# An mLSTM cell followed by a squared-ReLU feed-forward network: order of turning, weighting and transfers, and the place of one weight rounding

## The chip, the cores and the metric

The kernel runs on one core of a Trainium2 chip. The metric is the device time of one execution in microseconds (us); before the change it is 506.15 us as the median of six runs (504.21 to 507.88). TensorE multiplies matrices, VectorE (DVE in the profile), ScalarE (ACT) and GpSimd (POOL) work element by element, and SyncE (SP) issues nearly all transfers (DMAs). Each engine works through its own list of instructions in the order in which the kernel wrote them, and waits on semaphores for what other engines or transfers deliver.

## The reference

Two stages, in float32. The first is an mLSTM cell over 4 batches, 8 heads, 768 steps and a head dimension of 40:

```
m_new  = max(f[t] + m, i[t])
f_stab = exp(f[t] + m - m_new);  i_stab = exp(i[t] - m_new);  m = m_new
C = f_stab * C + i_stab * outer(v[t], k[t])
n = f_stab * n + i_stab * k[t]
y[t] = sigmoid(o[t]) * (C @ q[t]) / max(|n . q[t]|, 1)
```

The second takes the result as 3072 tokens of width 320 (batch and step as rows, head and dimension as columns):

```
h   = max(x @ w_in, 0)        # w_in  320 x 2048
out = (h * h) @ w_out         # w_out 2048 x 320
```

## The kernel before

**Chunks.** The recurrence is cut into 24 chunks of 128 steps (six for each batch), s = 0 to 23, each for all eight heads. Inside a chunk the cell is an attention with decays: the scores of keys against queries (`scores`, L445), times the weights exp(A + b) below the diagonal (`weighted`, L467, which multiplies the scores out of PSUM by the weights W and leaves P in W's place), then P times the values and the carried state C times the decayed queries (`attend_turned`, L542, L551 and L561).

**What a chunk needs.** `load_A` (L352) broadcasts a row of accumulated decays from DRAM to all 128 partitions, 512 KB in one transfer, into one of two buffers A_bc; `decays` (L387, ScalarE) takes its exponential for the queries, `mask` (L377, GpSimd) cuts the upper triangle, `weigh` (L401, ScalarE, eight exponentials) makes W. Keys and queries are needed turned, dimension on the partitions. From chunk 7 on this goes by way of DRAM: `pair_up` (L305, four transfers) copies k and q into rows, `load_squares` (L327, four transfers) reads them back as 32 x 32 squares into one of two buffers kqT, and `turn_kq` (L334, VectorE) turns every square. `scale_q` (L515) multiplies the queries by the decays.

**After a chunk.** `store_num` (L580) writes the numerators to DRAM and `load_num` (L585, four transfers) reads them back turned; `normalise_turned` (L597 to L606) divides and gates; `store_rows` (L632) and `load_rows` (L637) do the same for the result x, which `turn_squares` (L644) turns for the network.

**The network.** Tokens go in groups of two chunks, g = 0 to 11. Groups 0 and 1 take plain products (L674, L685); from group 2 on the first layer is done with a fast scheme of seven products over 2 x 2 blocks (`ffn1_begin`, `ffn1_open`, `ffn1_close`; L841, and L890 for the last 64 rows), and from group 1 on the second layer likewise (`ffn2_fast`, L765; sums on VectorE at L760, L781). In `ffn1_open` VectorE adds two products out of PSUM (L873, L875), in `ffn1_close` TensorE adds further products into the same banks, and VectorE ends with L908 to L911.

**Weights.** w_in and w_out come as 64-bit words and are rounded to float32 in 18 pieces by `Rounding`: `words` on ScalarE (L210, L212), `join` on VectorE (L221, L225, L226) and GpSimd (L230), each `join` also issuing the transfer of a later piece (L200). `step` does one `join` and keeps `words` one piece ahead.

**The order.** The schedule is written out by hand. A first loop, u = 0 to 7, does chunks 2 to 5 with the first layer of groups 0 and 1; `NEXT[u]` says how many pieces are rounded by the end of each u, and `WIN_SUMS` adds sums of weights after it (u = 7: L826). The second loop goes over units n, four for each chunk: `s = 6 + n // 4`, `at = n % 4`. `parts` gives each unit a quarter of a layer of the network: four quarters of the second layer, or (`fast`) of the first. `LAST[n]` is the number of rounded pieces by the end of unit n. Even chunks from 8 on do the scores of two chunks: their own at at = 0 and those of the next, odd one at at = 1. At at = 1 the transfers on SP are written in a row; at at = 2 others follow. Chunks 6 and 7 use a simpler order of transfers than chunks from 8 on.

Of the kernel before, what the change touches and what calls it, by code (L numbers as in the profile page):

```python
# [29 lines left out]
def kernel(  # L30
# [259 lines left out]
    def load_parts(s):  # L290
        d = st.setdefault(s, {})
        kq, va = d["kq"], d["va"] = kq_b[s % NKQ], va_b[s % NKQ]
        return (kq[:, 0, :, :D], k), (kq[:, 1, :, :D], q), (va[:, :, :D], v)
# [42 lines left out]
    def load_o(s):  # L336
        b, c = divmod(s, NB)
        r, (s0, s1) = next((r, (a, z)) for r, (a, z) in enumerate(RUNS) if a <= s < z)
        if s == s0:
            st["og", r] = ld.tile([P, 4, H, D], F32, name="og")  # L340
        og = st.setdefault(s, {})["og"] = st["og", r][:, s - s0]
        nc.sync.dma_start(og, o_gate[b, :, c * P : (c + 1) * P, :].rearrange("h p d -> p h d"))

    def sigmoid(s):
        nc.scalar.activation(st[s]["og"], st[s]["og"], AF.Sigmoid)
# [71 lines left out]
    def bank(o=False):  # L417
        if o == "h":
            t = ps_h.tile([P, W], F32, name="h_ps")
        else:  # L420
            t = ps_o.tile([P, W], F32, name="tp", tag="o_ps") if o else ps_at.tile([P, W], F32, name="tp", tag="at")
        return t[:].rearrange("p (j t) -> p j t", j=PR)
# [12 lines left out]
    def scores(s, o=(False, False)):  # L435
        d = st[s]

        sc = [bank(o[i]) for i in range(2)]
        d["sc"] = sc
        if s >= KQ_SQ:  # L440
            for j in range(PR):
                for keys in HALVES:
                    for i in range(2):
                        rows = slice(DP * i, DP * i + D)
                        nc.tensor.matmul(  # L445
                            sc[i][keys, j, :], lhsT=d["kT"][rows, j, keys], rhs=d["qT"][rows, j, :], start=(j == 0),
                            stop=True, skip_group_check=True,
                        )
            return
        for j in range(PR):  # L450
            for i in range(2):
                rows = slice(DP * i, DP * i + D)
                nc.tensor.matmul(  # L453
                    sc[i][:, j, :], lhsT=d["kT"][rows, j, :], rhs=d["qT"][rows, j, :], start=True, stop=True,
                )

    def weighted(s):
        d = st[s]
        d["P"] = []
        for i in range(2):  # L460
            heads = slice(i, H, 2) if s < KQ_SQ else slice(PR * i, PR * (i + 1))
            t = d["W"][:, heads, :]
            if s < W_IN:
                at = 2 * H * P + W * (2 * (s % 2) + i)
                t = flat_c[:, at : at + W].rearrange("p (j t) -> p j t", j=PR)
            d["P"].append(t)
            nc.vector.tensor_tensor(t, d["sc"][i], d["W"][:, heads, :], op=ALU.mult)  # L467
# [410 lines left out]
    def ffn1_rows(g, q, first):  # L878
        xT, xs = st["xT", g], st["xs"]
        X, Y, V, Z = st["f1"]  # L880
        lo, hi = HALVES
        pairs = (
            ((X, lo, xT[lo, 0, 2, :], False), (Y, hi, xT[hi, 1, 2, :], first)),
            ((V, lo, xT[lo, 1, 2, :], first), (Z, hi, xs[hi, 1, :], False)),
        )
        for pair in pairs:
            for n in range(4):
                for cols in HALVES:
                    for to, rows, rhs, start in pair:
                        nc.tensor.matmul(  # L890
                            to[cols, n, :], lhsT=w_in2[rows, 4 * q + n, cols], rhs=rhs,
                            start=(start and n == 0), stop=True, skip_group_check=True,
                        )
# [29 lines left out]
    def do(f, s):  # L923
        if 0 <= s < NT:
            f(s)

    def score(s):
        scores(s)
        weighted(s)


    zeros = consts.tile([P, 16], BF16)
    nc.vector.memset(zeros[:], 0.0)
# [12 lines left out]
    def load_part(s, i):  # L946
        b, c = divmod(s, NB)
        dst, src = load_parts(s)[i]
        nc.sync.dma_start(dst, src[b, :, c * P : (c + 1) * P, :].rearrange("h p d -> p h d"))
# [60 lines left out]
    rounding.step()  # L1010


    NEXT = (5, 8, 10, 11, 12, 13, 14, 15)
    WIN_SUMS = {5: 0, 6: 1, 7: 3}
    for u in range(8):
        s = 2 + u // 2
# [45 lines left out]
        if u < 4:  # L1062
            load_o(4 + u)
        while rounding.done < NEXT[u]:
            rounding.step()
# [17 lines left out]
    for g in range(1, NG):  # L1083
        parts += [(2, g, i) for i in range(4)]
        if g + 2 < NG:
            parts += [(1, g + 2, i) for i in range(4)]
    LAST = (16, 17, 18, 18, 18)
    assert LAST[-1] == len(pieces)
    for n, (which, g, i) in enumerate(parts):
        s, at = 6 + n // 4, n % 4  # L1090
        if n == 5:
            brought.close()
            late = ctx.enter_context(tc.tile_pool(name="late", bufs=1, side="right"))
        even = s >= 8 and s % 2 == 0
        fast = which == 1
        if at == 0:
            if s < 8 or even:
                do(score, s)
            if even:
                do(turn_kq, s + 1)  # L1100
        if at == 1:
            if even:
                do(lambda s: scores(s, ("h", "h")), s + 1)
            if fast:
                ffn1_rows(g, 0, True)
            do(attend_turned, s)
            do(decays, s + 1)
            do(mask, s + 1)
            if n > 4 and not even and not fast:
                do(turn_kq, s + 1)  # L1110
            do(decay_C, s + 1)
            if s > X_SQ and not fast:
                do(turn_squares, s - 1)
            do(store_num, s)
            if s >= 8:
                do(load_A, s + 2)
                do(lambda s: load_part(s, 0), s + 4)
                do(load_num, s)
                if not even:
                    do(load_squares, s + 2)  # L1120
                do(lambda s: load_part(s, 2), s + 4)
                if s < 20:
                    load_o(s + 4)
            else:
                do(load, s + 4)
                do(load_num, s)
            do(pair_up, s + 3)
        if 5 <= n < 8:
            sums_of_weights(n - 5)
        if n == 6:  # L1130
            sums(1, slice(0, NPAIR), (1, 2))
        if n == 8:
            sums_of_weights(3)
            sums(1, slice(0, NPAIR), (3,))
        if n == 9:
            sums(1, slice(0, NPAIR), (4,))
        if which == 2 and i == 3 and g == NG - 2:
            sums(g + 1, slice(0, NPAIR), (2,))
        if which == 2 and g > 1 and i < 2:
            sums(g, slice(0, NPAIR), (3 + i,))  # L1140
        if n == 0:
            ffn1_begin(g)
            sums_of_x(g)
            sums_of_win(2)
        if at == 3 and s >= 8 and s % 2 == 0 and s // 2 - 1 < NG:
            sums_of_x(s // 2 - 1)
        if at == 2 and not fast:
            if n > 4:
                do(scale_q, s + 1)
        if at == 3:  # L1150
            if s % 4 == 3:
                for r in range(s + 1, min(s + 5, NT)):
                    sigmoid(r)
        if fast:
            if i % 2:
                ffn1_close(g, i // 2, i == 1)
                if at == 1 and g > 2:
                    do(turn_kq, s + 1)
                    do(turn_squares, s - 1)
            else:  # L1160
                ffn1_open(g, i // 2)
                if i == 0 and g > 2:
                    sums(g - 1, slice(0, NPAIR), (2,))
            if at == 2 and g > 2:
                do(scale_q, s + 1)
        elif g == 0:
            ffn2(g, *divmod(i, 2))
        else:
            ffn2_fast(g, i)
        if at == 2:  # L1170
            do(lambda s: weigh(s, masked=True), s + 1)
            ffn1_square()
            if n < 4:
                do(turn_kq, s + 1)
                do(scale_q, s + 1)
            if even:
                do(weighted, s + 1)
            do(normalise_turned, s)
            do(store_rows, s)
            if s < 8 or even:  # L1180
                do(load_squares, s + 2)
            do(load_rows, s)
            if s < 8:
                do(load_A, s + 2)
        if at == 0:
            ffn1_square()
        if n < 5:
            while rounding.done < LAST[n]:
                rounding.step()
# [30 lines left out]
```

## Time and profile before

| what | value |
|---|---|
| median of six runs | 506.15 us |
| the profiled execution | 504.89 us |
| its span, first to last instruction | 503.1 us |
| TensorE matmul busy | 492.7 us (98%) |
| VectorE busy | 351.5 us (70%) |
| ScalarE busy | 249.0 us (49%) |
| GpSimd busy | 115.8 us (23%) |
| 16 DMA engines busy, SP's queue | 64.1% |
| granted TensorE clock | 1.0 |

The profile is of one execution. Times in it run from the first instruction. A line such as L334 is the line of the kernel text whose instruction is meant. PE is TensorE, PEld its weight loads, SPq SyncE's queue, on which each row is the issue of transfers and not their duration. Idle time of an engine is put down to the instruction or transfer that ended it. The page's row of the busy tenths shows TensorE at 9 in nearly all of the 40 slices after the first; the wall between the loops lies at some 97 us, chunk 8 begins at 137 us, and after 437 us only products of the second layer are left.

### The profile page before, as it was taken

To read this page: it belongs to the slowest core of one execution; us is meant where nothing else is said; L and a number is where in the kernel's file an instruction comes from. 1 tells how busy PE (TensorE), PEld (TensorE's weight loads), DVE (VectorE), ACT (ScalarE), POOL (GpSimd) and SP (SyncE) were. 2 spreads that over 40 slices of the span, in tenths; PEclk is the share of its full clock that TensorE was granted. 3 is DMA by queue.
4 is the path that set the end of the run, shared out by engine and by line. 5 is a ranking of instruction groups with operands and counts; after the bars stand their busy time and mean duration, and the time that the engine had idled before them with its cause. 6 is when DMAs were issued, how large, how long until landed. Compare 5 with 4: busy or idle time off the path is not lost.

```text
span 503.1 us, 13823 instructions
## 1 busy us (share of the span) xinstructions
PE 492.7 (98%) x5640; PEld 456.9 (91%) x5641; DVE 351.5 (70%) x646; ACT 249.0 (49%) x492; POOL 115.8 (23%) x138
## 2 busy tenths in 40 slices
PE   9988999989999999999999999999999999999997
PEld 4877878887689999999999999999999999999997
DVE  8588968779976776686876866767867856735441
ACT  3867888763532651672651680551771650423400
POOL 3356743232313021013013031013013030020000
PEclk9999999999999999999999999999999999999999
DMA  9999899855577867767867867867864622200000
GB/s 187 210 232 216 240 216 176 209 98 98 147 153 143 155 149 141 152 154 141 150 154 142 165 151 131 163 146 139 159 159 84 147 60 59 75 15 14 1 27 26
DMA packets 238238, 67.74 MB, mean 135 GB/s; under 512 B 185600, under 2 KB 232704, under 8 KB 238176
## 3 DMA queue, kind: packets, MB, share of 16 engines
q1 hardware_dynamic: 238080, 66.68, 64.1%
q8 instruction: 44, 0.72, 0.6%
q10 hardware_dynamic: 96, 0.20, 0.1%
q14 instruction: 18, 0.15, 0.1%
HBM read 54.56 MB, written 17.86 MB: 144 GB/s over the span
## 4 chain that ended last, share of the span: by engine, by line
PE 90%; DVE 5%; DMA 2%; ACT 1%; issue 1%; SPq 1%; POOL 0%; DVEq 0%; POOLq 0%
PE h_ps L765 33%; PE h_ps L841 25%; PE h_ps L890 8%; PE h_ps L674 4%; PE numT L551 4%; PE hp L490 2%; PE h_ps L445 2%; PE tp L445 1%; PE numT L542 1%; PE idle L938 1%; PE h_ps L685 1%; PE tp L453 1%; PE dC L483 1%; DMA va<-in_v_dram 1%; PE tp L430 1%; PE h_ps L711 1%
## 5 line engine op out<-in xcount | busy, mean ns | idle before, releaser
L377 POOL TENSOR_SCALAR_AFFINE_SELECT A_bc<-A_bc 128x1024 f32<-128x1024 f32 x22 | 25.9, 1176 | 134.3 <-ACT kq L387 86.4
L765 PE MATMUL h_ps<-T,S 128*128 128x160 f32 x352 | 51.4, 299 | 0.0
L871 ACT COPY r_sb<-h_ps 128x512 f32<-128x512 f32 x18 | 10.5, 585 | 80.1 <-PE h_ps L841 80.1
L765 PE MATMUL h_ps<-w_out,g 128*128 128x160 f32 x336 | 49.2, 303 | 0.0
L765 PEld LDWEIGHTS h_ps<-T,S 128*128 128x128 f32 x352 | 49.0, 190 | 0.0
L765 PEld LDWEIGHTS h_ps<-w_out,g 128*128 128x128 f32 x336 | 46.1, 190 | 1.4 <-issue 1.2
L401 ACT ACTIVATE A_bc<-A_bc,b_T 128x128 f32<-128x128 f32 x144 | 44.0, 389 | 4.2 <-POOL A_bc L377 3.9
L781 DVE TENSOR_TENSOR y_sb<-y_sb,h_ps 128x160 f32<-128x160 f32 x44 | 14.1, 320 | 43.5 <-PE h_ps L765 43.3
L841 PE MATMUL h_ps<-lent_t,w_in 128*128 128x128 f32 x320 | 42.5, 276 | 1.4 <-DVE r_sb L873 1.4
L841 PE MATMUL h_ps<-xT,w_in 128*128 128x128 f32 x320 | 42.8, 278 | 0.0
L841 PEld LDWEIGHTS h_ps<-lent_t,w_in 128*128 128x128 f32 x320 | 38.9, 192 | 1.6 <-DVE r_sb L873 1.6
L841 PEld LDWEIGHTS h_ps<-xT,w_in 128*128 128x128 f32 x320 | 38.9, 192 | 1.1 <-issue 0.7
L890 PE MATMUL h_ps<-xT,w_in 64*64 64x128 f32 x960 | 39.4, 273 | 0.0
L841 PE MATMUL h_ps<-lent_t 128*128 128x128 f32 x320 | 39.0, 275 | 0.0
L841 PEld LDWEIGHTS h_ps<-lent_t 128*128 128x128 f32 x320 | 37.3, 192 | 0.0
L890 PEld LDWEIGHTS h_ps<-xT,w_in 64*64 64x64 f32 x960 | 34.6, 133 | 2.4
L568 DVE STREAM_TRANSPOSE tn<-numT 128x256 f32<-128x256 f32 x36 | 15.8, 449 | 25.8 <-PE numT L551 25.8
L413 POOL TENSOR_TENSOR vw<-va,A_bc 128x328 f32<-128x328 f32 x15 | 11.9, 794 | 83.9 <-issue 40.5
L674 PE MATMUL h_ps<-xT,w_in 128*128 128x256 f32 x128 | 29.6, 383 | 1.2 <-POOL w_in L230 0.6
L908 DVE TENSOR_TENSOR r_sb<-r_sb,h_ps 128x512 f32<-128x512 f32 x20 | 13.7, 686 | 20.7 <-PE h_ps L841 14.3
L674 PEld LDWEIGHTS h_ps<-xT,w_in 128*128 128x128 f32 x128 | 23.6, 190 | 5.0 <-POOL w_in L230 1.0
L765 PE MATMUL h_ps<-w_out,g_c 128*128 128x160 f32 x192 | 28.0, 302 | 0.0
(188 smaller groups left out, 1078.6 us busy)
## 6 DMA issues: line engine op xcount, KB each, us to landing
A_bc<-a_rows SPq DMA_DIRECT2D x22, 512.0 KB, 5.3
num_rows<-tn SPq DMA_DIRECT2D x18, 256.0 KB, 2.6
kq<-num_rows SPq DMA_DIRECT2D x72, 64.0 KB, 3.4
raw<-in_moe_w_out_dram SPq DMA_DIRECT2D x7, 640.0 KB, 4.4
kqT<-kq_rows SPq DMA_DIRECT2D x34, 128.0 KB, 3.4
kq<-in_k_dram SPq DMA_DIRECT2D x24, 160.0 KB, 5.6
va<-in_v_dram SPq DMA_DIRECT2D x24, 160.0 KB, 4.2
og<-in_o_gate_dram SPq DMA_DIRECT2D x24, 160.0 KB, 3.5
```

The source lines that it names most:

```text
L377: nc.gpsimd.affine_select(A[:], A[:], compare_op=ALU.is_ge, fill=-1e30, base=0, pattern=[[0, H], [1, P]], channel_multiplier=-1,)
L401: nc.scalar.activation(d["W"][:, i * n + h, :], A[i][:, h, :], AF.Exp, bias=b_T[:, b, c, i * n + h : i * n + h + 1],)
L413: nc.gpsimd.tensor_tensor(d["vw"][:], d["va"][:], d["W"][:, :, P - 1 : P].to_broadcast([P, H, D1]), op=ALU.mult,)
L445: nc.tensor.matmul(sc[i][keys, j, :], lhsT=d["kT"][rows, j, keys], rhs=d["qT"][rows, j, :], start=(j == 0), stop=True, skip_group_check=True,)
L551: nc.tensor.matmul(numT[i][halves[g], e, :], lhsT=va_w[s % NKQ][:, h * D1 : h * D1 + DP], rhs=d["P"][h % 2][:, h // 2, :] if s < KQ_SQ els ...
L568: nc.vector.transpose(to[:, 2 * i : 2 * i + 2], numT[i][:, :2, :].rearrange("p c t -> p (c t)"))
L674: nc.tensor.matmul(hs[i][:, n, :], lhsT=w_in[:, a, fb * P : (fb + 1) * P], rhs=xT[:, :, a, :], start=(n == 0 and a == 0), stop=False,)
L765: nc.tensor.matmul(to, lhsT=lhsT[:, p], rhs=rhs[:, p, :], start=(start and p == 0), stop=(p == NPAIR - 1), skip_group_check=True,)
L781: add = lambda to, a, b: nc.vector.tensor_tensor(to, a, b, op=ALU.add)
L841: nc.tensor.matmul(to[:, n, :], lhsT=lhsT[:, 4 * q + n, :], rhs=rhs, start=(start and n == 0), stop=True, skip_group_check=True,)
L890: nc.tensor.matmul(to[cols, n, :], lhsT=w_in2[rows, 4 * q + n, cols], rhs=rhs, start=(start and n == 0), stop=True, skip_group_check=True,)
L908: tt(U2[:], U2[:], Y[:], op=ALU.add)
```

## The change

Four edits, all in the order of instructions:

- `NEXT[7]` is 16 in place of 15 and `LAST[0]` is 17 in place of 16: one step of rounding is written at the end of u = 7, so that units 0 and 2 have one each and unit 1 has none.
- In even chunks from 8 on, `turn_kq(s + 1)` stands between `scores(s)` and `weighted(s)`, not behind both (`score`, a helper that called both, is gone).
- In chunks from 8 on, `load_A(s + 2)` is issued behind `load_part(s + 4, 0)`, `load_num(s)` and, in odd chunks, `load_squares(s + 2)`, not ahead of them.
- Chunk 7 takes the order of transfers that the later odd chunks have: its `load_squares(9)` and `load_A(9)` are issued at at = 1, not at at = 2, and its v behind them.

```diff
-    def score(s):
-        scores(s)
-        weighted(s)
...
-    NEXT = (5, 8, 10, 11, 12, 13, 14, 15)
+    NEXT = (5, 8, 10, 11, 12, 13, 14, 16)
...
-    LAST = (16, 17, 18, 18, 18)
+    LAST = (17, 17, 18, 18, 18)
...
         if at == 0:
             if s < 8 or even:
-                do(score, s)
+                do(scores, s)
             if even:
                 do(turn_kq, s + 1)
+            if s < 8 or even:
+                do(weighted, s)
...
             do(store_num, s)
-            if s >= 8:
-                do(load_A, s + 2)
+            if s > 6:
                 do(lambda s: load_part(s, 0), s + 4)
                 do(load_num, s)
                 if not even:
                     do(load_squares, s + 2)
+                do(load_A, s + 2)
                 do(lambda s: load_part(s, 2), s + 4)
-                if s < 20:
+                if 8 <= s < 20:
                     load_o(s + 4)
             else:
                 do(load, s + 4)
...
-            if s < 8 or even:
+            if s < 7 or even:
                 do(load_squares, s + 2)
             do(load_rows, s)
-            if s < 8:
+            if s < 7:
                 do(load_A, s + 2)
```

## The prediction

> **What bounds the kernel now.** I read the page's busy times first, then the list of waits for the matmul engine alone, then the timelines round its two late waits on all queues, and last one steady pair of chunks, to see what margin the moved work has.
>
> ```profile
> PE 492.7 (98%) x5640; PEld 456.9 (91%) x5641; DVE 351.5 (70%) x646; ACT 249.0 (49%) x492; POOL 115.8 (23%) x138
> ```
>
> TensorE is busy for 492.7 of 503.1 us. The diff adds and removes no matmul and leaves the matmuls in their order, so only idle TensorE time can be won. The waits of TensorE, with what ended them:
>
> ```profile
> PE h_ps L841 <- DVE r_sb L873: 1.4, 1, 1.4
> PE tp L652 <- ACT g L698: 1.2, 1, 1.2
> PE dC L483 <- DVE g_c L467: 1.1, 1, 1.1
> ...
> PE h_ps L445 <- DVE kqT L334: 0.8, 1, 0.8
> ```
>
> All nine rows of that list add up to 7.3 us. L652, L483, both L674 and the start-up idle lie before 66 us, ahead of every edit. Two are left within reach: the first and the last shown. After 144 us no row is left. The first, on VectorE and then TensorE (start, duration, instruction, idle before and its releaser):
>
> ```profile
> 109.50 0.68 DVE L911 TENSOR_TENSOR g_c<-r_sb,h_ps 128x512 f32<-128x512 f32 x1
> 110.10 0.49 DVE L221 TENSOR_SCALAR mag<-mag 128x640 f32<-128x640 f32 x1
> 110.62 0.49 DVE L225 TENSOR_SCALAR mag<-mag 128x640 int32<-128x640 int32 x1
> 111.15 0.82 DVE L226 SCALAR_TENSOR_TENSOR mag<-raw,mag 128x640 int32<-128x640 int32 x1
> 111.89 0.68 DVE L873 TENSOR_TENSOR r_sb<-h_ps,r_sb 128x512 f32<-128x512 f32 x1
> 112.63 1.16 PE L841 MATMUL h_ps<-lent_t,w_in 128*128 128x128 f32 x8 [1.39 <-DVE r_sb L873]
> ```
>
> Unit 1's rounding (L221 to L226) stands ahead of the addition L873, which must have read its PSUM bank before TensorE may add to it. The second, at chunk 8, with the transfer queue (SPq) first:
>
> ```profile
> 128.30 1.75 SPq L585 DMA_DIRECT2D kq<-num_rows  x4
> ...
> 136.40 2.94 SPq L327 DMA_DIRECT2D kqT<-kq_rows  x4
> ...
> 142.43 0.47 SPq L352 DMA_DIRECT2D A_bc<-a_rows  x1
> 138.52 1.29 DVE L467 TENSOR_TENSOR A_bc<-tp,A_bc 128x512 f32<-128x512 f32 x2 [1.18 <-PE tp L445]
> 142.47 1.25 DVE L334 STREAM_TRANSPOSE kqT<-kqT 128x1024 f32<-128x1024 f32 x1 [2.66 <-DMA kqT<-kq_rows]
> 143.77 1.16 PE L445 MATMUL h_ps<-kqT 40*64 40x128 f32 x30 [0.83 <-DVE kqT L334]
> ```
>
> Chunk 9's squares are issued at 136.40, land after 142, VectorE waits 2.66 us to turn them, and TensorE, done with its products at 142.94, waits 0.83.
>
> **What the Trainium skill says.** "PSUM — Partial Sum Buffer", section Engine vs sequencer instructions: the queues of ScalarE, VectorE and GpSimd are strictly first in, first out, and matmuls start in program order. Both waits above are of this kind. "DMA: Bandwidth & Descriptors", section Anatomy of one DMA: a semaphore is waited for on the issuing sequencer, before dispatch. So what stands behind a waiting issue on SP waits too; here L585 starts at 128.30, 3.8 us after its chunk's store at 124.49. The same page, section Queues, rings and completion order: each DMA engine consumes a ring in order. That store had the 512 KB broadcast of A (issued 122.81) in front of it; the median landing of such a store is 2.6 us. This agrees, without being proof.
>
> **The rounding, worked out.** The step that unit 0 did goes to the end of u = 7; unit 0 then does the one that unit 1 did, and unit 1 does none. In unit 1, VectorE loses 0.49 + 0.49 + 0.82 us; by starts it is 111.89 - 110.10 = 1.79. L873 then starts at 110.10 and ends at 110.8, before TensorE comes at 111.24: the wait of **1.39** goes entirely, with 0.4 to spare. Where the step lands:
>
> ```profile
> 93.63 1.22 DVE L826 TENSOR_TENSOR lent_t<-w_in,lent_t 128x1024 f32<-128x1024 f32 x1
> 96.94 1.29 DVE L467 TENSOR_TENSOR A_bc<-tp,A_bc 128x512 f32<-128x512 f32 x2 [2.10 <-PE tp L453]
> ```
>
> VectorE waits 2.10 us before L467 for the scores; the step takes 1.8 to 1.9, so L826 moves to 95.5 and L467 stays. On ScalarE its two passes (0.81 + 0.79, starts 0.7 apart, so 1.4) come at 93.7, after L704, where 1.55 us of idle wait for the matmul L685 to end at 95.3. Their raw piece was issued at 85.51 (median landing 4.4 us). GpSimd's addition (1.54) falls into its idle from 93.5 to 105. Cover gone by half a microsecond: L826's sum is not read before 106.5, but L698's ReLU may free PSUM that TensorE takes at 96.8; at worst 0.5 us. I take 0; range 0 to +0.5.
>
> What is late next: chunk 7's weighting (L467) ended at 122.80 against TensorE's L551 at 122.84, no margin. TensorE will come at 121.45. VectorE: L873 and L875 to 111.5, L334 to 112.75, L515 to 113.45, L597 to L606 (1.7) to 115.15, the remaining rounding 1.8 to 116.95, L908 to L911 2.4 to 119.35, L467 to 120.6. Margin 0.85. The reload of the numerators that L597 needs has all landed by 112.6, so it does not wait.
>
> **Chunk 7's transfers.** All on SP. The four squares of chunk 9 leave their place behind x_sb (136.40) for that behind L585; the broadcast of A for chunk 9 follows them (was 142.43), then v (0.67), the four kq_rows and the output. L585 starts about 126.3: its store moves with TensorE to 123.1 and takes 3.2, less than the 3.8 above because A for chunk 8 is issued some 2 us sooner, behind an x_sb that is sooner. L585 takes 1.75 and the squares 2.94: issued from 128.1 to 131.0. From first issue to last landing they took 6 us before (136.40 to 142.4), which gives 134.1. VectorE reaches the turn at 135.8, and TensorE wants the scores at 142.94 - 1.39 = 141.55, so even 5 us more would be hidden: the **0.83** goes. What has been pushed back: kq_rows, from 130.1 to 132.1, are read by squares issued at 159; the output, 2 us later, holds one of three y_sb. A for chunk 9 is issued 11 us sooner. All 0.
>
> **Turning kq first in even chunks.** Nothing is added: 1.24 us (L334) and 1.28 (L467) swap. Chunk 12 is the tightest:
>
> ```profile
> 216.30 1.28 DVE L467 TENSOR_TENSOR A_bc<-tp,A_bc 128x512 f32<-128x512 f32 x2
> 217.50 1.23 DVE L334 STREAM_TRANSPOSE kqT<-kqT 128x1024 f32<-128x1024 f32 x1
> 218.83 1.22 PE L445 MATMUL h_ps<-kqT 40*64 40x128 f32 x32
> ```
>
> L334 ends at 218.73 and TensorE starts at 218.83: the margin, about 0, becomes 1.2. The added wait is L467's, behind L334; L467 now ends at 218.8, and L551 wants it at 219.98, 1.2 to spare. In chunk 14 the turn runs at 254.20; TensorE's scores come at 256.08 and L551 at 257.55. Gain: 0 to 0.1 in this execution; I take 0.
>
> **A's broadcast behind the squares.** For odd chunks it is issued behind four squares, for even ones behind four loads of the numerators:
>
> ```profile
> DMA to landing us min/median/max: 4.1/5.3/7.1
> ```
>
> Chunk 13: the squares now end at 250.2, less A's own slot 249.8, so A for chunk 15 lands at 255.1, at worst 256.9; ScalarE reads it at 257.57 (L387). Chunk 14: issued at 265.5, lands at 270.8, at worst 272.6; L387 runs at 271.42. It can be 1.2 us late there; behind it on ScalarE stands L907 at 278 and the exponentials at 281.7, on GpSimd the mask (1.09). That cover is 5 us. Cost 0. Squares and numerators come 0.4 to 2 us sooner, which VectorE does not need.
>
> **Sum.** 1.39 + 0.83 = 2.2 us of the profiled execution: span 503.1 to 500.9, its time 504.89 to 502.7. Its 504.89 lies 1.26 below the median of the runs, so I subtract from the median: 506.15 - 2.2 = **503.9**.
>
> **Rivals.** (1) Only one gap closes. For it: margins of 0.4 and 0.85 us behind the first, and ring congestion for the second. Against it: the squares have 6 us. 506.15 - 1.39 or - 0.83 gives 504.8 to 505.3, some 505.0. (2) More than the sum: other executions, longer than the profiled one, meet chunk 12's missing margin and late squares with longer waits, which both edits remove; another 1.3 us, the whole distance of median to profile, gives 502.6. The steady part shows no waits at all, which speaks against it. (3) Slower: the turn stands ahead of the weighting and waits for squares on VectorE, and L551 waits behind it. In chunk 14 the turn must start by 257.55 - 1.28 - 1.24 = 255.0, and the last square, issued at 248.46, lands at 251.7 with the median of 3.2 us that the tile's own view gives, at 253.5 with its longest, 5.0. It decides from 1.5 to 3.3 us later than that; 0.5 us beyond it in each of the eight even chunks 8 to 22 cost 4 us: 506.15 - 2.2 + 4 = 508. Against it: the squares go out sooner, with A out of their way. (4) The change does nothing: the waits are found elsewhere with the same size; part of (1).
>
> **How the numbers follow.** Forecast 0.66 with its own range 503.2 to 504.7; (1) and (4) 0.15; (2) 0.08; (3) and what I have not seen 0.11. What a measurement of this kernel can tell from no change is 0.3%, 1.5 us: faster means below 504.6. Of the forecast 0.84 lies there, of (1) a quarter, of (2) all: 0.55 + 0.04 + 0.08, some 0.66. Within: 0.11 + 0.11 + 0.02 = 0.24. Slower 0.10. The range cuts off half of (2) and all of (3): 502.4 to 505.9.
>
> **What would show it.** Right: no rounding between L911 and L873 in unit 1 and no TensorE wait for r_sb; chunk 9's squares issued before 132 and the scores of chunk 9 without a wait; nothing new in TensorE's list after 96 us. Wrong: L841 or L551 waiting between 96 and 124 us (L698 or L467 late), or rows of TensorE waiting for A_bc (L467) in even chunks, which would be (3).

## The result and the profile after

| | before | after |
|---|---|---|
| median of runs | 506.8 us (34 runs) | 510.13 us (15 runs) |
| ratio to before, 95% interval | | 1.0068 (1.0047 to 1.009) |
| the profiled execution | 504.89 us | 509.44 us |
| its span | 503.1 us | 507.7 us |

The change makes the kernel slower by 0.7%. The forecast was 503.9 us, with a range from 502.4 to 505.9: the sign is wrong. In the profiled execution TensorE's granted clock was about half (0.51) from 40.5 to 47.4 us, ahead of every edit; at chunk 6 this execution stands 2.2 us behind the profile of before, and I count from there. (The profiles of e1, e2 and e12 below, which beat both kernels, have such a stretch too, so it isn't the cause.)

The helper that went makes most line numbers above 926 smaller by four in the kernel after: its loads of k and v are L945, where the kernel before has L949.

**Where the time went.** The start of the product of P and the values (L551) is a mark in every chunk. Its time in the timeline, after minus before:

| chunk | 6 | 7 | 8 | 12 | 15 | 16 | 17 | 19 | 20 | 21 | 23 |
|---|---|---|---|---|---|---|---|---|---|---|---|
| us | +2.20 | +0.42 | -0.57 | -0.82 | -0.82 | -0.48 | +2.28 | +2.28 | +3.90 | +4.54 | +4.54 |

Up to chunk 12 the kernel gains 3.02 us: both gaps closed, and a little more. From chunk 15 to 21 it loses 5.36, all of it in two places, around chunk 16 and around chunk 20.

The list of TensorE's waits, kernel after (engine, tile and line, what ended the wait: total us, times, longest):

```profile
PE h_ps L765 <- ACT y_sb L785: 1.2, 1, 1.2
...
PE h_ps L765 <- DVE y_sb L781: 1.0, 2, 0.8
PE h_ps L765 <- DVE g_c L909: 0.9, 1, 0.9
```

The waits for r_sb (L873) and kqT (L334) are gone. Three new rows stand in their place, all in the second layer of the network (L765), which no edit touches. How much they are can be read from the busy time by stretch, from the L551 of one chunk to that of the next; kernel after, chunks 16 to 17, then 19 to 20:

```profile
294.64:315.71 21.07, 19.02 (x228) 18.18 (x225) 13.09 (x26) 10.37 (x20) 7.07 (x7) 1.00 0.61 145
352.53:373.42 20.89, 19.82 (x293) 18.87 (x289) 14.54 (x28) 9.64 (x19) 1.21 (x2) 1.00 0.74 140
```

Columns: the stretch and its length, then busy us and instructions of PE, PEld, DVE, ACT and POOL, clock, DMA share, GB/s. The same stretches of the kernel before are 18.31 and 19.26 us long, and TensorE is busy for all of them. After, it stands still 21.07 - 19.02 = 2.05 and 20.89 - 19.82 = 1.07 us, at full clock. Its busy time also grows, by 0.71 and 0.56 us for the same matmuls. Over all four stretches from chunk 15 to 17 and from 19 to 21, 3.3 us of the 5.36 are standstill and 2.0 are longer busy time. The ends of matmuls are modelled in the profile, and I leave that part open.

**What is behind the new waits.** All engines' waits, kernel after, the rows in which a transfer is late:

```profile
DVE xT L644 <- DMA xT<-x_rows: 22.7, 7, 5.2
ACT og L345 <- DMA og<-in_o_gate_dram: 16.9, 3, 6.9
DVE dm L597 <- DMA kq<-num_rows: 10.2, 5, 3.5
```

In the kernel before the same three rows have 7.3, 4.0 and 6.3 us, and none waits longer than 2.4 us at once. So three kinds of transfer are late that carry nothing of A: x turned for the network, the output gate, the numerators turned. A itself hardly is: its first readers on GpSimd and ScalarE (L377, L387) wait 14.3 us for it in sum, before 11.7, and neither row ends in a wait of TensorE. The timeline of after around chunk 16 leads from there to TensorE:

```profile
296.06 0.47 ACT L345 ACTIVATE og<-og 128x320 f32<-128x320 f32 x1 [6.91 <-DMA og<-in_o_gate_dram]
296.92 0.28 ACT L785 COPY y_sb<-h_ps 128x160 f32<-128x160 f32 x1
297.25 4.61 PE L765 MATMUL h_ps<-w_out,g_c 128*128 128x160 f32 x32 [1.22 <-ACT y_sb L785]
304.03 0.58 DVE L644 STREAM_TRANSPOSE xT<-xT 128x384 f32<-128x384 f32 x1 [5.24 <-DMA xT<-x_rows]
307.05 2.44 PE L765 MATMUL h_ps<-w_out,S 128*128 128x160 f32 x16 [0.83 <-DVE y_sb L781]
```

ScalarE's sigmoid waits 6.91 us for the output gate; the copy out of PSUM (L785) stands behind it in ScalarE's order, and TensorE waits for the bank. Seven microseconds later VectorE has waited 5.24 us for x, with L781 behind it, and TensorE waits again.

**Why they are late: the queue that issues them.** SP's timeline over one chunk (15), kernel before:

```profile
278.26 0.38 SPq L580 DMA_DIRECT2D num_rows<-tn  x1
278.74 0.40 SPq L352 DMA_DIRECT2D A_bc<-a_rows  x1
279.23 0.66 SPq L949 DMA_DIRECT2D kq<-in_k_dram  x1
281.22 1.75 SPq L585 DMA_DIRECT2D kq<-num_rows  x4
...
288.07 1.45 SPq L305 DMA_DIRECT2D kq_rows<-in_k_dram  x2
...
291.75 0.54 SPq L632 DMA_DIRECT2D x_rows<-x_sb  x1
```

and kernel after (left out are the four squares, v, o gate and the two rows of q):

```profile
280.65 0.38 SPq L580 DMA_DIRECT2D num_rows<-tn  x1
281.12 0.41 SPq L945 DMA_DIRECT2D kq<-in_k_dram  x1
283.42 2.62 SPq L585 DMA_DIRECT2D kq<-num_rows  x4
...
288.77 0.51 SPq L352 DMA_DIRECT2D A_bc<-a_rows  x1
...
291.16 2.57 SPq L305 DMA_DIRECT2D kq_rows<-in_k_dram  x2
...
295.79 0.53 SPq L632 DMA_DIRECT2D x_rows<-x_sb  x1
```

Between these two stores SP is nearly never idle: one issue follows another, but for one hole, in front of L585. There SP waits until the numerators that it has just stored have landed. Before, A was issued inside this hole. After, the hole is there all the same (L585 starts 2.77 us behind its store, before 2.96), empty but for k, and A's 0.51 us stand behind it. And A's 512 KB are now directly ahead of v, o gate and kq_rows: the first two issues of kq_rows take 2.57 us in place of 1.45. From the store of the numerators to that of x the same ten rows of transfers take 15.14 us, before 13.49. Nothing else holds the store of x: its data are ready at 289.41 (L606), 6.4 us earlier; before 287.59 and 4.2 us.

SP's own waits between 160 and 400 us, before and after:

```profile
SPq L585 <- DMA num_rows<-tn: 13.9, 13, 1.9
...
SPq L632 <- DVE y_sb L781: 7.1, 4, 2.9
```

```profile
SPq L585 <- DMA num_rows<-tn: 25.6, 13, 3.2
...
SPq L632 <- DVE y_sb L781: 2.4, 3, 1.3
```

The waits for a landing grow by 12 us. SP's reserve is the time in which it could issue but has to wait for an engine's result. I count it as SP's idle time in front of its stores of results (L580, L632, L801; gaps above 0.15 us), summed from the trace between 160 and 400 us: it shrinks from 10.7 to 2.1 us. In these 240 us SP issues for 187 (after: 183).

### The profile page after: what moved, and what is told of

It reads as the page before. It is cut to its first block, busy times and chain, and to the rows that moved or that the text cites. A ratio compares the mean times of both kernels' runs of the same rounds, so it can differ in the third digit from the quotient of the medians.

```text
span 507.7 us, 13829 instructions
## 1 busy us (share of the span) xinstructions
PE 497.5 (98%) x5640; PEld 460.9 (91%) x5641; DVE 352.3 (69%) x646; ACT 249.6 (49%) x492; POOL 118.6 (23%) x138
## 4 chain that ended last, share of the span: by engine, by line
PE 82%; DVE 6%; SPq 4%; DMA 3%; ACT 3%; issue 2%; POOL 0%; DVEq 0%; POOLq 0%
PE h_ps L765 28%; PE h_ps L841 23%; PE h_ps L890 7%; PE h_ps L711 3%; PE numT L551 3%; PE h_ps L674 3%; PE hp L490 2%; PE idle L934 1%; PE tp L445 1%; PE h_ps L445 1%; PE numT L542 1%; DMA num_rows<-tn 1%; PE tp L453 1%; SPq L585 1%; SPq L327 1%
## 5 line engine op out<-in xcount | busy, mean ns | idle before, releaser
L377 POOL TENSOR_SCALAR_AFFINE_SELECT A_bc<-A_bc 128x1024 f32<-128x1024 f32 x22 | 25.3, 1152 | 143.9 <-ACT kq L387 127.3
L765 PE MATMUL h_ps<-T,S 128*128 128x160 f32 x352 | 51.6, 299 | 1.0 <-DVE g_c L909 0.9
L765 PEld LDWEIGHTS h_ps<-T,S 128*128 128x128 f32 x352 | 49.0, 190 | 1.4 <-PE h_ps L765 1.1
L765 PE MATMUL h_ps<-w_out,g 128*128 128x160 f32 x336 | 49.2, 303 | 0.0
L765 PEld LDWEIGHTS h_ps<-w_out,g 128*128 128x128 f32 x336 | 46.1, 190 | 1.4 <-issue 1.2
L841 PE MATMUL h_ps<-xT,w_in 128*128 128x128 f32 x320 | 42.8, 278 | 0.0
L841 PE MATMUL h_ps<-lent_t,w_in 128*128 128x128 f32 x320 | 42.3, 276 | 0.0
L841 PEld LDWEIGHTS h_ps<-xT,w_in 128*128 128x128 f32 x320 | 38.9, 192 | 1.0 <-issue 0.7
L841 PE MATMUL h_ps<-lent_t 128*128 128x128 f32 x320 | 39.1, 275 | 0.0
L841 PEld LDWEIGHTS h_ps<-lent_t,w_in 128*128 128x128 f32 x320 | 38.9, 192 | 0.1
L841 PEld LDWEIGHTS h_ps<-lent_t 128*128 128x128 f32 x320 | 37.3, 192 | 0.1
L781 DVE TENSOR_TENSOR y_sb<-y_sb,h_ps 128x160 f32<-128x160 f32 x44 | 14.0, 318 | 33.0 <-PE h_ps L765 32.8
L413 POOL TENSOR_TENSOR vw<-va,A_bc 128x328 f32<-128x328 f32 x15 | 14.0, 934 | 77.6 <-issue 46.2
L765 PE MATMUL h_ps<-w_out,g_c 128*128 128x160 f32 x192 | 28.0, 302 | 1.2 <-ACT y_sb L785 1.2
L908 DVE TENSOR_TENSOR r_sb<-r_sb,h_ps 128x512 f32<-128x512 f32 x20 | 13.7, 686 | 21.0 <-PE h_ps L841 14.3
L765 PEld LDWEIGHTS h_ps<-w_out,g_c 128*128 128x128 f32 x192 | 26.3, 190 | 1.9 <-ACT y_sb L785 1.3
```

The lines of the kernel that those rows point to most:

```text
L377: nc.gpsimd.affine_select(A[:], A[:], compare_op=ALU.is_ge, fill=-1e30, base=0, pattern=[[0, H], [1, P]], channel_multiplier=-1,)
L413: nc.gpsimd.tensor_tensor(d["vw"][:], d["va"][:], d["W"][:, :, P - 1 : P].to_broadcast([P, H, D1]), op=ALU.mult,)
L765: nc.tensor.matmul(to, lhsT=lhsT[:, p], rhs=rhs[:, p, :], start=(start and p == 0), stop=(p == NPAIR - 1), skip_group_check=True,)
L781: add = lambda to, a, b: nc.vector.tensor_tensor(to, a, b, op=ALU.add)
L841: nc.tensor.matmul(to[:, n, :], lhsT=lhsT[:, 4 * q + n, :], rhs=rhs, start=(start and n == 0), stop=True, skip_group_check=True,)
L908: tt(U2[:], U2[:], Y[:], op=ALU.add)
```

## The experiments

Three explanations were set against each other. (1) The output gate alone: it is issued behind A, lands late, and holds ScalarE. (2) SP's queue as a whole: A no longer fills the hole, so SP loses its reserve, and everything on it is late. (3) The order of turning and weighting, with which VectorE holds L551. Each diff is against the kernel after, where nothing else is said. The ratios, with their 95% intervals, are to runs of the kernel before that belong to the same group of experiments.

| run | what | median us | ratio |
|---|---|---|---|
| e1_A_first | after, A back in the hole | 503.55 | 0.9931 (0.9907 to 0.9955) |
| e2_o_before_A | after, o gate ahead of A | 502.52 | 0.9916 (0.989 to 0.9942) |
| e3_sigmoid_later | after, sigmoids later | 509.8 | 1.0066 (1.0047 to 1.0085) |
| e4_only_A | before, A's move alone | 514.02 | 1.0141 (1.0103 to 1.0179) |
| e9_kq_rows_last | after, kq_rows last | 515.73 | 1.0163 (1.0132 to 1.0194) |
| e10_kq_rows_last_sigmoid_later | e9 and e3 | 515.38 | 1.0155 (1.0127 to 1.0182) |
| e11_v_in_gap | after, v in the hole | 502.68 | 0.9926 (0.9901 to 0.995) |
| e12_o_v_in_gap | after, o gate and v in the hole | 502.94 | 0.9934 (0.9911 to 0.9958) |
| e13_tiny_transfers | e1, 48 more transfers on SP | 514.2 | 1.0154 (1.0129 to 1.018) |
| e5_only_rounding | before, rounding alone | 504.89, one execution | |
| e6_only_chunk7 | before, chunk 7 alone | 505.39, one execution | |
| e7_only_turn | before, turn alone | 507.34, one execution | |

**A back in the hole.**

```diff
             if s > 6:
+                if s >= 8:
+                    do(load_A, s + 2)
                 do(lambda s: load_part(s, 0), s + 4)
                 do(load_num, s)
                 if not even:
                     do(load_squares, s + 2)
-                do(load_A, s + 2)
+                if s < 8:
+                    do(load_A, s + 2)
```

> The changed kernel with one edit undone: from chunk 8 on the broadcast of A is issued first in its row again. Theory 1 (A's place makes the last o gate of chunks 11, 15 and 19 late, and ScalarE's sigmoid holds its queue) and theory 2 (A's place makes SP run late as a whole): both expect 2 to 3 us less than before, ratio 0.994 to 0.997, ScalarE waiting for the o gate under 2 us at each of the three places. Rival 3 (the turn ahead of the weighting costs the time): as slow as the changed kernel, ratio 1.005 to 1.009.

503.55 us: with the other three edits kept, the kernel is 0.7% faster than before and 6.6 us faster than after. TensorE has no wait behind 67 us. By L551 it gains 3.03 us from chunk 6 to 23 (+1.59 to -1.44 against before). On SP, chunk 15 goes from the store of the numerators (276.66) to that of x (289.13) in 12.47 us, against 15.14 in the kernel after. So the place of A behind the squares makes the loss. This doesn't tell (1) from (2).

**The output gate ahead of A.**

```diff
                 do(load_num, s)
                 if not even:
                     do(load_squares, s + 2)
+                if 8 <= s < 20:
+                    load_o(s + 4)
                 do(load_A, s + 2)
                 do(lambda s: load_part(s, 2), s + 4)
-                if 8 <= s < 20:
-                    load_o(s + 4)
```

> The changed kernel, with the o gate's load moved ahead of the broadcast of A; A stays behind squares and numerators. Theory 1: the o gate lands before ScalarE comes, the waits of 3.4, 6.9 and 6.6 us fall below 2 us, TensorE's waits after 290 us go, ratio 0.994 to 0.998. Theory 2: SP's row stays late, x_rows and numerators land as late as in the changed kernel, ratio 1.003 to 1.009 although the o gate is early. Rival 3: 1.005 to 1.009.

502.52 us, as good as A in the hole, and again no wait of TensorE behind 67 us. The hole stays without A here. ScalarE's waits for the gate fall to 2.9 us, but VectorE's for x are still 16.5, against 22.7 in the kernel after. SP still waits 19.3 us for the numerators' store (after: 25.6), and its reserve is 7.5 us in place of 2.1. Taken alone this speaks for (1).

**The sigmoids later.** The order on SP is that of the kernel after; the four sigmoids go from the end of chunks 11, 15 and 19 to the second unit of the chunk that follows.

```diff
         if at == 3:
-            if s % 4 == 3:
+            if s == 7:
...
+        if at == 1 and s > 8 and s % 4 == 0:
+            for r in range(s, min(s + 4, NT)):
+                sigmoid(r)
```

> The changed kernel with all transfers as they are, but the four sigmoids of chunks 12, 16 and 20 written two units later (second unit of the next chunk), so that ScalarE does not come before the o gate has landed. Theory 1: the wait for the o gate falls to 0, ratio 0.994 to 0.999. Theory 2: no better than the changed kernel, 1.003 to 1.009, with VectorE still waiting over 3 us for xT or numerators near 288, 304 and 366 us.

509.8 us, the same as after: with ScalarE's wait for the gate gone, the time is lost all the same. VectorE's waits for x are 25.7 us in sum, more than in the kernel after. The timeline at the first loss, which has moved to chunk 12:

```profile
214.98 3.87 SPq L305 DMA_DIRECT2D kq_rows<-in_k_dram  x2
220.22 0.53 SPq L632 DMA_DIRECT2D x_rows<-x_sb  x1
227.89 0.58 DVE L644 STREAM_TRANSPOSE xT<-xT 128x384 f32<-128x384 f32 x1 [6.89 <-DMA xT<-x_rows]
```

x is ready at 213.17 (the end of L606) and is stored at 220.22, because v, the gate and kq_rows are issued in between, the two rows of k alone for 3.87 us; nearly 15 us after it was ready VectorE gets it back. TensorE's wait of 2.13 us at 231.29 is for the sums L781 behind it. Explanation (1) falls as the only way: the gate is one way from SP to TensorE, x another.

**A's move alone.** From the kernel before, with its order of turning, rounding and chunk 7:

```diff
             if s >= 8:
-                do(load_A, s + 2)
                 do(lambda s: load_part(s, 0), s + 4)
                 do(load_num, s)
                 if not even:
                     do(load_squares, s + 2)
+                do(load_A, s + 2)
```

> The kernel before with one edit alone: from chunk 8 on the broadcast of A behind numerators and squares. Theories 1 and 2: about 5 us slower than before (what the changed kernel lost after 288 us), ratio 1.007 to 1.013, with waits for the o gate of 3 to 7 us at three places. Rival 3: no difference, 0.998 to 1.002.

514.02 us. By L551 it loses 7.2 us between chunks 6 and 23 (+0.92 to +8.11), without the turn being moved: (3) isn't the cause. The same two transfers are late as in the kernel after: VectorE waits 27.0 us for x, up to 5.7 at once, and ScalarE 16.6 for the gate, up to 6.3.

**kq_rows last in their chunk, alone and with later sigmoids.** If the four slow issues of kq_rows hold the store of x, x should come sooner with kq_rows behind it.

```diff
                 do(load_num, s)
-            do(pair_up, s + 3)
+            if s < 8:
+                do(pair_up, s + 3)
...
                 do(load_A, s + 2)
+            if s >= 8:
+                do(pair_up, s + 3)
```

> The changed kernel, with the four kq_rows transfers of chunks from 8 on issued last in their chunk (behind x_rows and xT), so that SP does not stand at them with A, v and the o gate in front while x_sb is ready. The o gate still stands behind A. If the row of SP alone costs the time: VectorE's waits for xT (22.7 us in the changed kernel) fall to under 9 us, TensorE waits for nothing after 144 us, ratio 0.991 to 0.997. If the o gate alone costs it: ScalarE's waits of 3 to 7 us stay and the ratio is 1.003 to 1.009. If both do: between, 0.997 to 1.003.

> The two together: kq_rows last, and the sigmoids of chunks 12, 16 and 20 two units later. Both ways of A's place to TensorE are closed, so 0.991 to 0.997 if these two are all; over 1.000 if A itself (its mask and exponentials) is late, or if the sigmoids' new place costs by itself.

515.73 and 515.38 us: neither expectation came true, both kernels are slower than after by 1%. VectorE's wait for the numerators in the first:

```profile
DVE dm L597 <- DMA kq<-num_rows: 26.4, 9, 4.8
```

x does come sooner (VectorE waits 16.4 us for it in place of 22.7), but kq_rows now stand ahead of the next chunk's store of numerators, and VectorE's wait for these grows from 10.2 to 26.4. As far as these waits show, the lateness has been passed on, not removed. My expectation looked at one transfer and not at the queue, which is the prediction's mistake over again.

**Something else in the hole.** If (2) is right, A may stay behind the squares as long as another transfer fills the hole.

```diff
                 do(lambda s: load_part(s, 0), s + 4)
+                do(lambda s: load_part(s, 2), s + 4)
                 do(load_num, s)
                 if not even:
                     do(load_squares, s + 2)
                 do(load_A, s + 2)
-                do(lambda s: load_part(s, 2), s + 4)
```

> The changed kernel with v's load moved from behind A to ahead of the numerators' loads, where SP waits for the store of the numerators to land (15.0 us in all between 160 and 400 us before, 27.0 in the changed kernel). A stays behind numerators and squares. If the time is lost because A's issue no longer fills that wait and SP has no slack left: the wait falls to 17 to 22 us, x_rows is stored less late, ratio 0.994 to 1.000; the o gate, still behind A, may leave up to 2 us on TensorE. If only A's bytes ahead of the o gate and kq_rows matter: as slow as the changed kernel, 1.003 to 1.009.

502.68 us, with the output gate still behind A. SP's own waits between 160 and 400 us:

```profile
SPq L632 <- DVE y_sb L781: 12.8, 5, 3.1
SPq L585 <- DMA num_rows<-tn: 12.6, 13, 2.0
```

The wait for the numerators is back at 12.6 us (after: 25.6), and SP has reserve again: it waits 12.8 us for the results of L781 alone. ScalarE still waits 8.3 us for the gate, up to 4.0 at once, and TensorE doesn't feel it. A's 512 KB still go out ahead of the gate and of kq_rows here, so its bytes ahead of these don't make the loss by themselves. With the output gate in the hole too, ahead of v,

```diff
                 do(lambda s: load_part(s, 0), s + 4)
+                if 8 <= s < 20:
+                    load_o(s + 4)
+                do(lambda s: load_part(s, 2), s + 4)
                 do(load_num, s)
...
-                do(lambda s: load_part(s, 2), s + 4)
-                if 8 <= s < 20:
-                    load_o(s + 4)
```

> As the last, with the o gate too ahead of the numerators' loads. SP's slack and the early o gate together: no wait of TensorE after 144 us, ratio 0.990 to 0.996. Over 1.000 if the numerators, now behind two loads of 160 KB, come late in turn.

it is 502.94 us: no wait for the gate at all, 2.4 us for x, the wait for the numerators' store down to 3.9 us and SP's reserve up to 28.8, and no gain over the others: from chunk 6 to 23 e1, e2, e11 and e12 all gain 3.0 us by L551. Once SP isn't late, making it earlier brought nothing here.

**The queue's time by itself.** Does SP's time alone do it, without A's 512 KB in another place? The fast kernel with A in the hole (e1) gets four more transfers in each of chunks 8 to 19, of 8 bytes each from DRAM to DRAM; nobody reads them. The diff is against e1; the 48 destinations are left out.

```diff
                 do(load_num, s)
+                if 8 <= s < 20:
+                    for _ in range(4):
+                        nc.sync.dma_start(tiny.pop(), f_gate[0, 0:1, 0:2])
```

> The fast version with A first, and in chunks 8 to 19 four more transfers of 8 bytes each behind the numerators' loads: SP's time without bytes. About 0.4 us each, 1.5 us a chunk and 18 us in all, against about 12 us that SP waits for x_sb and tn in that version. If SP's queue is the second bound: ratio 0.997 to 1.010, with x_rows stored later and the same waits of VectorE for xT and numerators as in the changed kernel. If bytes alone matter: 0.991 to 0.995, as without them.

514.2 us: 10.7 us (2.1%) slower than the same kernel without them; the direction was expected, the size is beyond what I had expected. The view of these transfers' line, then one of SP's own waits between 160 and 400 us:

```profile
L1121 SPq DMA_DIRECT2D tiny<-in_f_gate_dram x48: 544/556/670, 151.1 to 369.4; - x48
```

```profile
SPq L1121 <- DMA kq<-in_k_dram: 1.5, 4, 0.5
```

An issue takes 0.556 us (the line gives shortest, median and longest in ns), so 26.7 us over twelve chunks, 2.2 a chunk; the kernel without them had 12.0 us of reserve in 240 us. The same three transfers are late as in the kernel after: 21.8 us for x, 12.0 for the gate, 19.6 for the numerators. So an overfull queue is enough to give the picture, with A where it was; the added time is larger than what A's move takes, so the sizes can't be compared. A smaller part is landings: the second view shows 8-byte transfers waiting for the load of k, and the squares wait 2.1 us for that of the numerators, though neither needs the other's data. In both cases it is the transfer eight issues earlier in the queue's order whose landing is waited for, and in the trace the two share a semaphore: all of SP's transfers take eight semaphores in turn.

**The reserve, run by run.** By the same count the kernels that lose have 2.1 us (after), 0 (e3), 1.6 (e4), 4.0 (e9) and 2.8 (e13) of reserve in the 240 us; those that don't have 6.6 us (e7) or more (before 10.7, e1 12.0, e2 7.5, e11 14.4, e12 28.8). That goes with explanation (2), but a kernel that is late for another reason would show little reserve too; only e13 takes time from the queue and leaves the order as it was. (e10 is left out: its profiled execution took 522.47 us, far from its median.)

**The other three edits, each alone from the kernel before.**

```diff
-    NEXT = (5, 8, 10, 11, 12, 13, 14, 15)
+    NEXT = (5, 8, 10, 11, 12, 13, 14, 16)
...
-    LAST = (16, 17, 18, 18, 18)
+    LAST = (17, 17, 18, 18, 18)
```

> The kernel before with the rounding's move alone. Between the starts of L551 in chunks 6 and 7, 17.67 us in the kernel before and 15.89 in the changed one, it should show 15.9 to 16.3 and TensorE's wait for r_sb (1.4) gone; the later wait for kqT (0.8) stays. Nothing else moves by over 0.2 us after chunk 8.

From the L551 of chunk 6 to that of 7 it takes 15.88 us (106.40 to 122.28), before 17.67: 1.79 gained. TensorE's wait for r_sb is gone, that for kqT (0.9) is left. Against the expectation it loses 0.67 us between chunks 19 and 20.

```diff
-            if s >= 8:
-                do(load_A, s + 2)
+            if s > 6:
+                if s >= 8:
+                    do(load_A, s + 2)
                 do(lambda s: load_part(s, 0), s + 4)
                 do(load_num, s)
                 if not even:
                     do(load_squares, s + 2)
+                if s < 8:
+                    do(load_A, s + 2)
...
-            if s < 8 or even:
+            if s < 7 or even:
                 do(load_squares, s + 2)
             do(load_rows, s)
-            if s < 8:
+            if s < 7:
                 do(load_A, s + 2)
```

> The kernel before with chunk 7's order of transfers alone. TensorE's wait for kqT at chunk 8 (0.8) goes; between the starts of L551 in chunks 7 and 8, 22.50 us before, it should show 21.5 to 21.7. The wait for r_sb (1.4) stays.

From chunk 7 to 8 it takes 21.50 us (124.13 to 145.63), before 22.50: 1.00 gained. The wait for kqT is gone, that for r_sb (1.4) is left.

```diff
             if s < 8 or even:
-                do(score, s)
+                do(scores, s)
             if even:
                 do(turn_kq, s + 1)
+            if s < 8 or even:
+                do(weighted, s)
```

> The kernel before with the turn ahead of the weighting alone: no wait of TensorE added or removed but for chunk 8 (0.8, may grow by up to 0.5, since the weighting now stands behind the late squares) and up to 0.3 us less at chunk 12; so the span from chunk 9 on differs by under 0.6 us from the kernel before.

Against before, L551 stands at +2.57 us in chunk 7, +2.70 in chunk 8, +2.45 from chunk 12 on. Neither step can be put down to the turn: e4 and e5, which leave the turn where it was, have 0.13 and 0.11 more in chunk 8 too, and e4, e5 and e6 have 0.23 to 0.26 less in chunk 12. It is the profile of before that lost 0.25 there. What the turn is worth shows elsewhere: in e5 VectorE ends the turn at 367.76, behind the weighting, and TensorE's scores of chunk 20 start at 367.85. That is e5's loss of 0.67; e6 loses 0.45 at the same chunk in the same way. The profiles with the turn first and no late queue (e1, e2, e7, e11, e12) lose nothing after chunk 12. One execution each isn't enough to compare these three edits by their times.

Not tried: A's issue on another engine's queue, fewer and larger transfers on SP, and the sigmoids' later place with A in the hole.

## Why the prediction was wrong

**The step that failed** is the last of the working, "A's broadcast behind the squares", with its "Cost 0". It asked only who reads A and found 5 us of cover on ScalarE and GpSimd. That much held. It never asked what stands behind A on SP, nor how much SP has to spare. The runs showed in its place: A had filled a wait that stays when A leaves, the queue has some 0.8 us of reserve in a chunk (10.7 us over 13), and with A moved 2.1 of the 10.7 are left. Alone the move costs 7.2 us by L551 (e4), in the kernel after 5.36 by L551, and 6.6 us by the medians of after and e1. The sentence it was supported by, "Squares and numerators come 0.4 to 2 us sooner", shows how small the possible gain was: in chunk 15 the numerators are issued only 0.2 us sooner behind their store, because that store's landing decides, not A.

The rule was at hand. The prediction cites the Trainium skill, "DMA: Bandwidth & Descriptors", section Anatomy of one DMA (a semaphore is waited for on the issuing sequencer, before dispatch), and uses it for the loads behind chunk 7's store. The same rule, applied to L585 in chunks 8 to 20, says that a transfer moved from in front of a wait to behind it lengthens the queue by its own issue. The traces agree: SP's waits at L585 are 13.9 us before and 25.6 after. Even where the prediction priced this hole, in chunk 7, it did so wrongly: the loads were to start 3.2 us behind their store, and start 3.98 behind it (124.92 to 128.90), before 3.81. It cost nothing there, for the squares had time to spare.

**The sum, term by term.**

| step | forecast, us | measured, us | from |
|---|---|---|---|
| rounding out of unit 1 | -1.39 | -1.78 | L551, chunks 6 to 7 (e5: -1.79) |
| chunk 7's transfers | -0.83 | -1.0 | L551, chunks 7 to 8 (e6: -1.00) |
| turning first | 0 | -0.25, not the turn's alone | L551, chunks 8 to 12 (the same in e4, e5 and e6, without the turn) |
| A behind the squares | 0 | +5.36 | L551, chunks 15 to 21 |
| sum | -2.2 | +2.33 | |

Together with the 2.2 us by which the profiled execution was late at chunk 6 this gives 4.5, against 4.6 between the two spans. Both gaps were named rightly, with their mechanism. The first gain is the 1.79 us that the prediction had found for VectorE's rounding by starts, and not TensorE's listed wait of 1.39. L551 of chunk 7 starts 0.05 us after the weighting L467 ends, before (122.79 and 122.84) as after (123.22 and 123.27), as if VectorE set its time in both. The margin of 0.85 us that the prediction saw there is then 0.05: its working lets L875 follow L873 at once, and it comes 0.48 us later (before 0.46).

**The rivals.** Of rival (1), only one gap closed, nothing was seen. Rival (2), more than the sum, gives nearly the right size for the three other edits, 502.6 us against 503.55 in e1, and its reason has some support: the missing margin at an even chunk cost 0.25 us in the profile of before, 0.67 in e5 and 0.45 in e6. Rival (3), slower at 508, came nearest in time with the wrong mechanism: the turn waits for no squares that matter (e7), and TensorE has no row that waits for A_bc. In its words "Against it: the squares go out sooner, with A out of their way" the same blind spot is seen: A wasn't in the squares' way, since it stood in the wait ahead of them. The 0.11 for "(3) and what I have not seen" was too little for an edit on a queue whose load had not been added up.

**The signs it named.** Right: no rounding ahead of L873 in unit 1, no wait for r_sb, chunk 9's squares issued at 130.68, its scores without a wait. Wrong: "nothing new in TensorE's list after 96 us" - three rows of L765. The two signs given for a failure (L841 or L551 waiting by 124 us, A_bc in even chunks) didn't come; the failure came from where no sign had been set.

**What stays open.** How the 5.36 us split between SP's lost time and the late landings of the gate isn't settled. In e2 the gate alone is moved ahead of A, and all is gained back, though the hole stays without A and SP still waits 19.3 us for the numerators; in e3 the gate's wait is taken away, and nothing is gained. The two fit together if the queue stands close to the edge, so that a little decides; that is argued, not shown. Why e2's reserve is 5 us larger isn't shown either. Between 160 and 400 us its issues of k's rows take 22.7 us in sum, in the kernel after 30.1 (before 19.3), though A stands a few issues ahead of them in both. Also open is the longer busy time of TensorE, 2.0 of the 5.36 us.

## What to carry to other kernels

Before moving a transfer, add up the queue that issues it: its issues, its waits for landings, and what is left, per stage; a queue that issues for 187 of 240 us and waits for landings in another 24 is as much a serial engine as TensorE. A transfer that stands between a store and the load which waits for it took nearly no time of its own here; moved behind that load, it adds its issue to all that follows. So fill such a hole, and before you empty it see that the reserve can bear it (e2's could). Ask then who holds its engine while it waits for each of those followers (here the sigmoid on ScalarE, the turn of x on VectorE), for there the loss comes out, far from the edit.

## What the runs showed of the hardware

- A transfer of 8 bytes takes 0.556 us of SP's time in e13, about as much as a load of the output gate (0.58, 160 KB) and more than A's 512 KB in chunk 15 (0.40 before, 0.51 after): the issue's length doesn't follow the bytes.
- The length of an issue isn't fixed: the two issues of k's rows in a chunk took 1.45 us before, 1.39 in e1, 2.57 in after and 3.87 in e3. That A's 512 KB a few issues ahead cause it isn't shown: A is ahead of them in e2, e11 and e12 too, where they take 22.7, 20.9 and 17.6 us between 160 and 400 us, against 30.1 in after and 19.3 before. In e11 A's own issue is longer instead, 1.26 us in the median.
- The best four orders of transfers, with waits for the numerators' store from 3.9 to 19.3 us and a reserve from 7.5 to 28.8, lie between 502.5 and 503.6 us (e1, e2, e11, e12), while e4 and e9, with a reserve of 1.6 and 4.0, are at 514 and 516. In these kernels a busy queue cost nothing measurable while it had reserve.
- SP's transfers signal on eight semaphores in turn, and an issue can wait for the landing of the transfer eight issues earlier, whose data it doesn't need: in e13, between 160 and 400 us, four times each for the 8-byte transfers and the squares, up to 0.8 us.
